# Attention in pairs of heads, and a shorter clamp in the MLP, for a sliding-window attention + hard-swish MLP kernel

## The chip, the cores and the metric

The kernel runs on one core of a Trainium2 chip. Its time is the device time of one execution in microseconds (us). Each kernel was executed several times, and the text quotes the median. All runs compared here are fast; one run of the kernel before, at 1180.69 us, was not, and is left out. The profile is of one execution; its span (first to last instruction) is about 2 us below the time of that same execution.

Engine names: PE does matmuls and transposes (PEld is its weight load), DVE is the vector engine, ACT the scalar engine, POOL the GpSimd engine; SP's queue issues the loads. SBUF and PSUM are the two on-chip memories in which the kernel allocates tiles; its matmuls write to PSUM.

## The reference, cut to what matters

Attention of 8 batches x 8 heads, 576 positions, head size 64, each position seeing itself and the 127 before it, with a linear bias per head. Then an MLP (512 to 2048 to 512) on the 4608 tokens.

```python
scores = scale * q @ k.T                         # scale = 1/8
rel = pos[:, None] - pos[None, :]
mask = (rel >= 0) & (rel < 128)
scores = np.where(mask, scores - slopes[h] * abs(rel), -1e9)
attn = softmax(scores)
x = (attn @ v)                                   # then [tokens, heads * 64]
h = x @ w_in
g = h * np.clip(h + 3.0, 0.0, 6.0) / 6.0
out = g @ w_out
```

## The kernel before

Weights, biases (`add_tiles`, which also hold the mask) and the attention's result `xT` stay in SBUF. The sequence is cut into five tiles of 128 positions (the last has 64). Scores are computed transposed (keys on partitions), so that the exponentials can be weights of the value matmul; the softmax's sum comes from a column of ones beside v. The kernel is written one head at a time. A scheduler takes the program and builds an order of instructions for each engine, so the order that runs is not the order in the text.

```python
for b in range(B):
    for h in range(H):
        ...                                             # tiles qT kT vv ldf ldb (3 buffers), tps (2, PSUM)
        nc.vector.memset(vv[:, :], 1.0)                 # for the column of ones
        for kt_i in range(n_qt):
            nc.sync.dma_start(out=ldf[:sk, 0:D], in_=q[b, h, slc, :])         # k and v likewise
            nc.vector.tensor_scalar(out=ldb[:sk, 0:D], in0=ldf[:sk, 0:D], scalar1=scale, ...)
            nc.vector.tensor_copy(out=ldb[:sk, D:2 * D], in_=ldf[:sk, D:2 * D])
            nc.vector.tensor_copy(out=vv[:sk, ds(kt_i * (D + 1), D)], in_=ldf[:sk, 2 * D:3 * D])
            nc.tensor.transpose(tps[:, :sk], ldb[:sk, 0:D], ident[:sk, :sk])
            nc.vector.tensor_copy(out=qT[:, slc], in_=tps[:, :sk])
            ...                                         # the same for kT
        for qt in range(n_qt):
            for kt_i in ([qt] if qt == 0 else [qt - 1, qt]):
                nc.tensor.matmul(sc_ps[:sk, :sq], lhsT=kT[:, kslc], rhs=qT[:, qslc], ...)
                nc.vector.tensor_tensor(out=sc_ps[:sk, :sq], in0=sc_ps[:sk, :sq], in1=at, op=ALU.add)
                nc.scalar.activation(out=exp_sb[:sk, :sq], in_=sc_ps[:sk, :sq], func=ACT.Exp)
                nc.tensor.matmul(av_ps[:sq, :], lhsT=exp_sb[:sk, :sq], rhs=vv[...], ...)
            nc.vector.reciprocal(recip[:sq, :], av_ps[:sq, D:D + 1])
            nc.vector.tensor_scalar(out=av_sb[:sq, :], in0=av_ps[:sq, :D], scalar1=recip[:sq, :], ...)
            nc.tensor.transpose(avT_ps[:, :sq], av_sb[:sq, :], ident[:sq, :sq])
            nc.vector.tensor_copy(out=xT[...], in_=avT_ps[:, :sq])
...
for nt in range(n_nt):                                  # 9 token tiles of 512
    for ms in range(n_ms):                              # 16 slices of the hidden layer
        ...                                             # 4 matmuls into hT_ps
        nc.scalar.activation(out=r6, in_=hT_ps, func=ACT.Relu, bias=bias3[:, 0:1])
        nc.vector.tensor_scalar(out=r6, in0=r6, scalar1=6.0, scalar2=1.0 / 6.0, op0=ALU.min, op1=ALU.mult)
        nc.vector.tensor_tensor(out=gT, in0=hT_ps, in1=r6, op=ALU.mult)
        ...                                             # 4 matmuls, gT into the four out_ps
```

The softmax here doesn't subtract the row's maximum and nothing guards it: scores larger than these inputs give would overflow.

## Time and profile before

| | kernel before |
|---|---|
| time, median of 11 runs | 962.65 us (960.84 to 964.21) |
| span of the profiled run | 961.8 us |
| loads of weights, to the first transpose | 36.8 us |
| attention, first transpose to first MLP matmul | 650.4 us |
| MLP, to the last copy of a result | 271.7 us |
| tail | 2.9 us |
| DVE instructions per pair of heads | 100 |

Read the stages first. Attention is two thirds of the time, and DVE is the busiest engine there; in the MLP it is PE. A total over the run (PE 77%, DVE 74%) hides that. The lines are shown in the prediction.

To split DVE's time into work and waiting I use the trace's start times, not the durations, because neighbouring DVE instructions overlap. For each kind and shape of instruction, the lower quarter point of the gaps from its start to the next start is taken as its own cost; what a gap has beyond that is counted as waiting of the next instruction. In the 300 us from 100 to 400 us the kernel before has 200.7 us of own work and 99.3 of waiting over 29.6 heads: per two heads 13.6 and 6.7 us.

### The profile page before, as it was taken

Reading aid. Unit: us, or ns where it says so; the run is one execution under the profiler, and the core shown is the slowest. Engines: PE = TensorE matmul, PEld = TensorE weight load, DVE = VectorE, ACT = ScalarE, POOL = GpSimd, SP = SyncE. Lnnn points to the kernel's source line nnn. Section 1 sums busy time; section 2 is a strip of 40 time slices with the busy share of each in tenths; the row PEclk is TensorE's granted clock in tenths of the full one; section 3 lists DMA queues with packets and bytes.
Section 4 is the critical chain, followed back from the end, with each engine's and each line's share of the span. In section 5 each row is a group of like instructions: output and inputs, shape, how many; then the busy total and the mean of one; then the engine's idle time right before and its main releaser. Section 6 shows DMA issues by size and latency. Waiting matters only on the chain.

```text
span 961.8 us, 13507 instructions
## 1 busy us (share of the span) xinstructions
PE 743.8 (77%) x3264; PEld 342.0 (36%) x3264; DVE 713.6 (74%) x3563; ACT 249.6 (26%) x721; POOL 5.1 (1%) x24
## 2 busy tenths in 40 slices
PE   0277776777777777777777777777899999999996
PEld 0133333333333333333333333333333333333332
DVE  4577887888787887878887878888556666656665
ACT  0122221222222222222222222222233333433332
POOL 2000000000000000000000000000000000000000
PEclk9999999999999999999999999999999999999999
DMA  6421222122211221222222212221001111001111
GB/s 253 125 49 41 44 45 45 44 49 45 44 43 43 46 46 40 47 45 47 44 45 48 45 44 46 45 48 39 13 0 45 45 44 44 27 18 44 45 44 44
DMA packets 134094, 47.05 MB, mean 49 GB/s; under 512 B 126848, under 2 KB 126848, under 8 KB 133504
## 3 DMA queue, kind: packets, MB, share of 16 engines
q1 hardware_dynamic: 134016, 46.20, 18.6%
q8 instruction: 25, 0.41, 0.2%
q14 instruction: 53, 0.43, 0.2%
HBM read 36.70 MB, written 9.44 MB: 48 GB/s over the span
## 4 chain that ended last, share of the span: by engine, by line
PE 48%; DVE 31%; ACT 7%; issue 6%; DMA 6%; POOL 0%; DVEq 0%; SPq 0%; ACTq 0%; POOLq 0%
PE out_ps L181 14%; PE sc_ps L133 7%; DVE sc_ps L138 7%; PE av_ps L141 7%; PE avT_ps L152 6%; PE hT_ps L170 6%; PE tps L118 4%; ACT exp_sb L140 4%; PE tps L116 4%; DVE xT L153 4%; DVE qT L117 3%; DVE gT L179 3%; ACT r L175 3%; DVE kT L119 3%; DVE av_sb L148 2%
## 5 line engine op out<-in xcount | busy, mean ns | idle before, releaser
L140 ACT ACTIVATE exp_sb<-sc_ps 128x128 bf16<-128x128 f32 (+2 forms) x576 | 149.4, 264 | 500.6 <-DVE sc_ps L138 423.5
L141 PE MATMUL av_ps<-vv,exp_sb 128*128 128x65 bf16 (+2 forms) x576 | 138.2, 241 | 67.6 <-ACT exp_sb L140 55.9
L138 DVE TENSOR_TENSOR sc_ps<-sc_ps,add_tiles 128x128 f32<-128x128 f32 (+2 forms) x576 | 155.8, 275 | 34.0 <-PE sc_ps L133 23.5
L133 PE MATMUL sc_ps<-qT,kT 64*128 64x128 bf16 (+2 forms) x576 | 154.7, 274 | 23.4 <-DVE kT L119 10.9
L181 PE MATMUL out_ps<-w_out_sb,gT 128*128 128x512 bf16 x576 | 151.5, 381 | 5.0 <-DVE gT L179 1.4
L170 PE MATMUL hT_ps<-xT,w_in_sb 128*128 128x512 bf16 x576 | 151.4, 384 | 0.3 <-DVE xT L153 0.3
L175 ACT ACTIVATE r<-hT_ps,bias 128x512 f32<-128x512 f32 x144 | 98.9, 687 | 168.6 <-PE hT_ps L170 161.4
L116 PE MATMUL tps<-ident,ldb 128*64 128x128 bf16 (+1 forms) x320 | 95.3, 303 | 59.9 <-DMA ldf<-in_k_dram 36.8
L176 DVE TENSOR_SCALAR r<-r 128x512 f32<-128x512 f32 x144 | 60.4, 421 | 84.6 <-ACT r L175 83.9
L152 PE MATMUL avT_ps<-ident,av_sb 128*64 128x128 bf16 (+1 forms) x320 | 96.9, 303 | 31.7 <-DVE av_sb L148 29.6
L141 PEld LDWEIGHTS <-exp_sb 128*128 128x128 bf16 (+2 forms) x576 | 62.7, 109 | 151.2 <-ACT exp_sb L140 119.0
L118 PE MATMUL tps<-ident,ldb 128*64 128x128 bf16 (+1 forms) x320 | 90.8, 289 | 24.2 <-DVE qT L117 13.9
L179 DVE TENSOR_TENSOR gT<-hT_ps,r 128x512 bf16<-128x512 f32 x144 | 99.4, 691 | 13.3 <-DVE r L176 0.5
L153 DVE COPY xT<-avT_ps 64x128 bf16<-64x128 bf16 (+1 forms) x320 | 66.8, 209 | 34.0 <-PE avT_ps L152 23.9
L133 PEld LDWEIGHTS <-kT 64*128 64x128 bf16 (+1 forms) x576 | 59.0, 103 | 78.3 <-DVE kT L119 30.8
L148 DVE TENSOR_SCALAR av_sb<-av_ps,recip 128x64 bf16<-128x64 f32 (+1 forms) x320 | 86.0, 269 | 0.5
L170 PEld LDWEIGHTS <-w_in_sb 128*128 128x128 bf16 x576 | 56.9, 99 | 69.8 <-issue 3.3
L181 PEld LDWEIGHTS <-gT 128*128 128x128 bf16 x576 | 46.2, 97 | 95.7 <-DVE gT L179 58.5
L119 DVE COPY kT<-tps 64x128 bf16<-64x128 bf16 (+1 forms) x320 | 65.4, 206 | 18.7 <-PE tps L118 12.1
L117 DVE COPY qT<-tps 64x128 bf16<-64x128 bf16 (+1 forms) x320 | 65.4, 205 | 14.9 <-PE tps L116 9.8
L116 PEld LDWEIGHTS <-ldb 128*64 128x64 bf16 (+1 forms) x320 | 40.8, 128 | 95.8 <-DVE ldb L110 77.9
L152 PEld LDWEIGHTS <-av_sb 128*64 128x64 bf16 (+1 forms) x320 | 40.6, 127 | 76.3 <-DVE av_sb L148 58.7
(22 smaller groups left out, 327.5 us busy)
## 6 DMA issues: line engine op xcount, KB each, us to landing
out_dram<-osb SPq DMA_DIRECT2D x36, 256.0 KB, 2.2
ldf<-in_q_dram SPq DMA_DIRECT2D x256, 32.0 KB, 1.8
ldf<-in_k_dram SPq DMA_DIRECT2D x256, 32.0 KB, 1.8
ldf<-in_v_dram SPq DMA_DIRECT2D x256, 32.0 KB, 1.9
tmp<-in_moe_w_in_dram SPq DMA_DIRECT2D x4, 1024.0 KB, 8.0
tmp<-in_moe_w_out_dram SPq DMA_DIRECT2D x16, 256.0 KB, 3.7
ldf<-in_q_dram SPq DMA_DIRECT2D x64, 16.0 KB, 1.9
ldf<-in_k_dram SPq DMA_DIRECT2D x64, 16.0 KB, 1.9
```

What stands on the lines that cost most here:

```text
L116: nc.tensor.transpose(tps[:, :sk], ldb[:sk, 0:D], ident[:sk, :sk])
L118: nc.tensor.transpose(tps[:, :sk], ldb[:sk, D:2 * D], ident[:sk, :sk])
L133: nc.tensor.matmul(sc_ps[:sk, :sq], lhsT=kT[:, kslc], rhs=qT[:, qslc], start=True, stop=True)
L138: nc.vector.tensor_tensor(out=sc_ps[:sk, :sq], in0=sc_ps[:sk, :sq], in1=at, op=ALU.add)
L140: nc.scalar.activation(out=exp_sb[:sk, :sq], in_=sc_ps[:sk, :sq], func=ACT.Exp)
L141: nc.tensor.matmul(av_ps[:sq, :], lhsT=exp_sb[:sk, :sq], rhs=vv[:sk, ds(kt_i * (D + 1), D + 1)], start=first_mm, stop=(kt_i == qt))
L152: nc.tensor.transpose(avT_ps[:, :sq], av_sb[:sq, :], ident[:sq, :sq])
L153: nc.vector.tensor_copy(out=xT[p_off:p_off + D, ds(h_off + qt * QT, sq)], in_=avT_ps[:, :sq])
L170: nc.tensor.matmul(hT_ps, lhsT=w_in_sb[:, ds(ks * d_ff + ms * 128, 128)], rhs=xT[:, ds(ks * Ntok + nt * NT, NT)], start=(ks == 0), stop=(k ...
L175: nc.scalar.activation(out=r6, in_=hT_ps, func=ACT.Relu, bias=bias3[:, 0:1])
L179: nc.vector.tensor_tensor(out=gT, in0=hT_ps, in1=r6, op=ALU.mult)
L181: nc.tensor.matmul(out_ps[sub], lhsT=gT[:, ts(sub, 128)], rhs=w_out_sb[:, ts(ms, d_model)], start=(ms == 0), stop=(ms == n_ms - 1))
```

## The change

Its intent is to halve the number of small DVE instructions: two heads share each load, cast, transpose, score add, exponential, reciprocal, scaling and copy. The value part of a query tile is written one tile later ("late"), so that the scheduler has something to put in the gaps. In the MLP, scale and bias of the Relu do part of the clamp, and the rest goes into one instruction with the product: min(relu(h/6 + 0.5), 1) x h.

```diff
-            for h in range(H):
-                qT = ap.tile([D, S], BF16)
-                vv = ap.tile([128, n_qt * (D + 1)], BF16)
-                ldf = ap.tile([128, 3 * D], FP32)
-                tps = pp.tile([D, 128], BF16)
+            for hp in range(H // 2):
+                h0 = 2 * hp
+                qT = ap.tile([128, S], BF16)
+                vv = ap.tile([128, n_qt, 2, D + 1], BF16)
+                ldf = ap.tile([128, 3, 2, D], FP32)
+                tps = ppt.tile([128, 128], BF16)            # one buffer now (cut: kT, ldb)
...
-                    nc.sync.dma_start(out=ldf[:sk, 0:D], in_=q[b, h, slc, :])
+                        nc.sync.dma_start(out=ldf[:sk, _t, :, :],
+                                          in_=src[b, h0:h0 + 2, slc, :].rearrange("h s d -> s h d"))
...
-                        sc_ps = pp.tile([128, 128], FP32)
-                        nc.tensor.matmul(sc_ps[:sk, :sq], lhsT=kT[:, kslc], rhs=qT[:, qslc],
-                                         start=True, stop=True)
+                        sc_ps = ppsc.tile([128, 2, 512], FP32)
+                        for _h in range(2):
+                            po = _h * D
+                            nc.tensor.matmul(sc_ps[:sk, _h, :sq],
+                                             lhsT=kT[po:po + D, kslc],
+                                             rhs=qT[po:po + D, qslc],
+                                             start=True, stop=True)
...
-                        nc.vector.tensor_tensor(out=sc_ps[:sk, :sq], in0=sc_ps[:sk, :sq],
+                        nc.vector.tensor_tensor(out=sc_ps[:sk, :, :sq], in0=sc_ps[:sk, :, :sq],
                                                 in1=at, op=ALU.add)
...
+                    late.append(value)                      # value(): matmuls, reciprocal, scaling,
+                    while len(late) > 1:                    # transpose and copy of one query tile
+                        late.pop(0)()
...
-                nc.scalar.activation(out=r6, in_=hT_ps, func=ACT.Relu, bias=bias3[:, 0:1])
-                nc.vector.tensor_scalar(out=r6, in0=r6, scalar1=6.0, scalar2=1.0 / 6.0,
-                                        op0=ALU.min, op1=ALU.mult)
+                nc.scalar.activation(out=r6, in_=hT_ps, func=ACT.Relu,
+                                     bias=bias3[:, 0:1], scale=1.0 / 6.0)
-                nc.vector.tensor_tensor(out=gT, in0=hT_ps, in1=r6, op=ALU.mult)
+                nc.vector.scalar_tensor_tensor(out=gT, in0=r6, scalar=1.0, in1=hT_ps,
+                                               op0=ALU.min, op1=ALU.mult)
```

More of the change, by code (lines that the diff above doesn't have):

```diff
@@ L48 @@
     bias3 = perm.tile([128, 1], FP32)
-    nc.vector.memset(bias3, 3.0)
+    nc.vector.memset(bias3, 0.5)
     make_identity(nc, ident)
@@ L93 @@
     with tc.tile_pool(name="attn", bufs=3) as ap, \
-         tc.tile_pool(name="psum", bufs=2, space=bass.MemoryType.PSUM) as pp:
-        for b in range(B):
-            for h in range(H):
-                qT = ap.tile([D, S], BF16)
-                kT = ap.tile([D, S], BF16)
-                vv = ap.tile([128, n_qt * (D + 1)], BF16)
-                ldf = ap.tile([128, 3 * D], FP32)
-                ldb = ap.tile([128, 2 * D], BF16)
-                tps = pp.tile([D, 128], BF16)
-                nc.vector.memset(vv[:, :], 1.0)
+         tc.tile_pool(name="psum", bufs=2, space=bass.MemoryType.PSUM) as pp, \
+         tc.tile_pool(name="psc", bufs=2, space=bass.MemoryType.PSUM) as ppsc, \
+         tc.tile_pool(name="ptp", bufs=1, space=bass.MemoryType.PSUM) as ppt:
+        late = []
+        add3 = add_tiles[:, :].rearrange("p (t s) -> p t s", s=128)
+        for b in range(B):
+            for hp in range(H // 2):
+                h0 = 2 * hp
+                qT = ap.tile([128, S], BF16)
+                kT = ap.tile([128, S], BF16)
+                vv = ap.tile([128, n_qt, 2, D + 1], BF16)
+                ldf = ap.tile([128, 3, 2, D], FP32)
+                ldb = ap.tile([128, 2, 2 * D], BF16)
+                tps = ppt.tile([128, 128], BF16)
+                nc.vector.memset(vv[:, :, :, :], 1.0)
                 for kt_i in range(n_qt):
@@ L106 @@
                     slc = ds(kt_i * QT, sk)
-                    nc.sync.dma_start(out=ldf[:sk, 0:D], in_=q[b, h, slc, :])
-                    nc.sync.dma_start(out=ldf[:sk, D:2 * D], in_=k[b, h, slc, :])
-                    nc.sync.dma_start(out=ldf[:sk, 2 * D:3 * D], in_=v[b, h, slc, :])
-                    nc.vector.tensor_scalar(out=ldb[:sk, 0:D], in0=ldf[:sk, 0:D],
+                    for _t, src in enumerate((q, k, v)):
+                        nc.sync.dma_start(out=ldf[:sk, _t, :, :],
+                                          in_=src[b, h0:h0 + 2, slc, :].rearrange("h s d -> s h d"))
+                    nc.vector.tensor_scalar(out=ldb[:sk, 0, :], in0=ldf[:sk, 0, :, :].rearrange("p h d -> p (h d)"),
                                             scalar1=scale, scalar2=0.0,
                                             op0=ALU.mult, op1=ALU.add)
-                    nc.vector.tensor_copy(out=ldb[:sk, D:2 * D], in_=ldf[:sk, D:2 * D])
-                    nc.vector.tensor_copy(out=vv[:sk, ds(kt_i * (D + 1), D)],
-                                          in_=ldf[:sk, 2 * D:3 * D])
-                    nc.tensor.transpose(tps[:, :sk], ldb[:sk, 0:D], ident[:sk, :sk])
+                    nc.vector.tensor_copy(out=ldb[:sk, 1, :], in_=ldf[:sk, 1, :, :].rearrange("p h d -> p (h d)"))
+                    nc.vector.tensor_copy(out=vv[:sk, kt_i, :, 0:D], in_=ldf[:sk, 2, :, :])
+                    nc.tensor.transpose(tps[:, :sk], ldb[:sk, 0, :], ident[:sk, :sk])
                     nc.vector.tensor_copy(out=qT[:, slc], in_=tps[:, :sk])
-                    nc.tensor.transpose(tps[:, :sk], ldb[:sk, D:2 * D], ident[:sk, :sk])
+                    nc.tensor.transpose(tps[:, :sk], ldb[:sk, 1, :], ident[:sk, :sk])
                     nc.vector.tensor_copy(out=kT[:, slc], in_=tps[:, :sk])
-                h_off = (h // 2) * Ntok + b * S
-                p_off = (h % 2) * D
+                h_off = hp * Ntok + b * S
                 for qt in range(n_qt):
@@ L126 @@
                     qslc = ds(qt * QT, sq)
-                    av_ps = pp.tile([128, D + 1], FP32)
-                    first_mm = True
-                    for kt_i in ([qt] if qt == 0 else [qt - 1, qt]):
+                    kts = [qt] if qt == 0 else [qt - 1, qt]
+                    exps = []
+                    for kt_i in kts:
                         sk = min(QT, S - kt_i * QT)
                         kslc = ds(kt_i * QT, sk)
-                        sc_ps = pp.tile([128, 128], FP32)
-                        nc.tensor.matmul(sc_ps[:sk, :sq], lhsT=kT[:, kslc], rhs=qT[:, qslc],
-                                         start=True, stop=True)
+                        sc_ps = ppsc.tile([128, 2, 512], FP32)
[5 more added lines that the diff above has]
+                                             start=True, stop=True)
@@ L135 @@
                         typ = 0 if kt_i == qt else 1
-                        at = add_tiles[:sk, ds((typ * H + h) * 128, sq)]
-                        exp_sb = ap.tile([128, 128], BF16)
-                        nc.vector.tensor_tensor(out=sc_ps[:sk, :sq], in0=sc_ps[:sk, :sq],
+                        at = add3[:sk, typ * H + h0:typ * H + h0 + 2, :sq]
+                        exp_sb = ap.tile([128, 2, 128], BF16, bufs=6)
+                        nc.vector.tensor_tensor(out=sc_ps[:sk, :, :sq], in0=sc_ps[:sk, :, :sq],
@@ L139 @@
                                                 in1=at, op=ALU.add)
-                        nc.scalar.activation(out=exp_sb[:sk, :sq], in_=sc_ps[:sk, :sq], func=ACT.Exp)
-                        nc.tensor.matmul(av_ps[:sq, :], lhsT=exp_sb[:sk, :sq],
-                                         rhs=vv[:sk, ds(kt_i * (D + 1), D + 1)],
-                                         start=first_mm, stop=(kt_i == qt))
-                        first_mm = False
-                    recip = ap.tile([128, 1], FP32)
@@ L146 @@
-                    nc.vector.reciprocal(recip[:sq, :], av_ps[:sq, D:D + 1])
-                    av_sb = ap.tile([128, D], BF16)
-                    nc.vector.tensor_scalar(out=av_sb[:sq, :], in0=av_ps[:sq, :D],
-                                            scalar1=recip[:sq, :], scalar2=0.0,
-                                            op0=ALU.mult, op1=ALU.add)
-                    avT_ps = pp.tile([D, 128], BF16)
-                    nc.tensor.transpose(avT_ps[:, :sq], av_sb[:sq, :], ident[:sq, :sq])
@@ L153, with value @@
-                    nc.vector.tensor_copy(
-                        out=xT[p_off:p_off + D, ds(h_off + qt * QT, sq)],
-                        in_=avT_ps[:, :sq])
+                        nc.scalar.activation(out=exp_sb[:sk, :, :sq], in_=sc_ps[:sk, :, :sq],
+                                             func=ACT.Exp)
+                        exps.append((kt_i, sk, exp_sb))
+                    def value(exps=exps, qt=qt, sq=sq, vv=vv, h_off=h_off):
+                        av_ps = pp.tile([128, 2, D + 1], FP32, name="av_ps")
+                        for _h in range(2):
+                            for i, (kt_i, sk, exp_sb) in enumerate(exps):
+                                nc.tensor.matmul(av_ps[:sq, _h, :], lhsT=exp_sb[:sk, _h, :sq],
+                                                 rhs=vv[:sk, kt_i, _h, :],
+                                                 start=(i == 0), stop=(i == len(exps) - 1))
+                        recip = ap.tile([128, 2, 1], FP32, name="recip")
+                        nc.vector.reciprocal(recip[:sq, :, :], av_ps[:sq, :, D:D + 1])
+                        av_sb = ap.tile([128, 2, D], BF16, name="av_sb")
+                        nc.vector.tensor_tensor(out=av_sb[:sq, :, :], in0=av_ps[:sq, :, :D],
+                                                in1=recip[:sq, :, :].broadcast_to([sq, 2, D]), op=ALU.mult)
+                        avT_ps = ppt.tile([128, 128], BF16, name="avT_ps")
+                        nc.tensor.transpose(avT_ps[:, :sq], av_sb[:sq, :, :].rearrange("p h d -> p (h d)"),
+                                            ident[:sq, :sq])
+                        nc.vector.tensor_copy(out=xT[:, ds(h_off + qt * QT, sq)], in_=avT_ps[:, :sq])
@@ L157 @@
+                    late.append(value)
+                    while len(late) > 1:
+                        late.pop(0)()
+                while late:
+                    late.pop(0)()
     NT = 512
```

## The prediction

> **What bounds the kernel now.** I read the page's totals first, then a table of busy time by stage, the groups split by shape, the waits, and two stretches of the timeline. The totals:
>
> ```profile
> PE 743.8 (77%) x3264; PEld 342.0 (36%) x3264; DVE 713.6 (74%) x3563; ACT 249.6 (26%) x721; POOL 5.1 (1%) x24
> ```
>
> Taken alone they name no bound. The table by stage (stretch in us, its length, then busy time and count of PE, PE's weight loads, DVE, ACT and POOL, tensor clock, DMA share, GB/s) splits the run in two:
>
> ```profile
> 100.00:660.00 560.00, 416.32 (x1835) 207.44 (x1835) 454.46 (x2777) 129.88 (x500) 0.00 (x0) 1.00 0.20 45
> 700.00:962.00 262.00, 250.99 (x1107) 98.11 (x1105) 166.02 (x313) 94.81 (x138) 0.00 (x0) 0.99 0.10 37
> ```
>
> To 37.2 us the weights load. From there to 687.2 us is attention, 64 heads in 650.0 us; the MLP's nine token tiles follow, 29.38 us apart, to 951.6 us, and a tail of 10.2 us. In attention VectorE (DVE) is busy 81% of the time, PE 74%; in the MLP PE is busy 96% and DVE 63%. So the attention change must be read on DVE, the MLP change on PE.
>
> In attention DVE does 50 instructions a head; 2777 of them in 560 us make a head every 10.08 us. They are small:
>
> ```profile
> L138 DVE TENSOR_TENSOR sc_ps<-sc_ps,add_tiles 128x128 f32<-128x128 f32 x448 | 127.2, 289 | 21.0 <-PE sc_ps L133 13.6 <-PE av_ps L141 0.7 <-ACT exp_sb L140 0.7
> L148 DVE TENSOR_SCALAR av_sb<-av_ps,recip 128x64 bf16<-128x64 f32 x256 | 69.0, 270 | 0.5
> L117 DVE COPY qT<-tps 64x128 bf16<-64x128 bf16 x256 | 54.0, 211 | 8.0 <-PE tps L116 3.6
> L114 DVE CAST vv<-ldf 128x64 bf16<-128x64 f32 x256 | 46.3, 183 | 1.4 <-DMA ldf<-in_v_dram 0.6
> L146 DVE RECIPROCAL recip<-av_ps 128x1 f32<-128x1 f32 x256 | 41.4, 162 | 8.9 <-PE av_ps L141 4.9
> ...
> L138 DVE TENSOR_TENSOR sc_ps<-sc_ps,add_tiles 128x64 f32<-128x64 f32 x64 | 14.3, 224 | 3.5 <-PE sc_ps L133 1.9 <-PE avT_ps L152 0.5
> ```
>
> The mean of one is not what it costs the queue, since neighbours overlap. Start to start, where the next was ready, the trace has about 0.20 us for a 128x128 add (0.14 at 128x64), 0.10 for a 64-element cast, 0.14 for a 128-wide PSUM copy, 0.085 for a reciprocal, 0.19 for the scaling, 0.245 for the memset. Summed over a head: casts 15 x 0.10 = 1.5, qT/kT 1.33, adds 7 x 0.20 + 2 x 0.14 = 1.68, reciprocals 0.43, scalings 0.96, xT 0.90, memset 0.25; together 7.05 us. The other 3.0 us of the 10.08 are waits of this engine, on PE for the most part:
>
> ```profile
> DVE xT L153 <- PE avT_ps L152: 23.9, 86, 0.6
> DVE sc_ps L138 <- PE sc_ps L133: 23.5, 90, 0.7
> DVE kT L119 <- PE tps L118: 12.1, 40, 0.4
> DVE qT L117 <- PE tps L116: 9.8, 42, 0.4
> ```
>
> In the MLP the timeline (start us, us, engine, line, in brackets the idle time before and its releaser) shows what PE waits for, in every group of 24 matmuls:
>
> ```profile
> 701.05 2.32 PE L170 MATMUL hT_ps<-xT,w_in_sb 128*128 128x512 bf16 x10
> 701.47 0.69 ACT L175 ACTIVATE r<-hT_ps,bias 128x512 f32<-128x512 f32 x1 [3.13 <-PE hT_ps L170]
> 702.19 0.43 DVE L176 TENSOR_SCALAR r<-r 128x512 f32<-128x512 f32 x1 [2.07 <-ACT r L175]
> ...
> 702.72 0.69 DVE L179 TENSOR_TENSOR gT<-hT_ps,r 128x512 bf16<-128x512 f32 x1
> ...
> 703.46 0.55 PEld L181 LDWEIGHTS <-gT 128*128 128x128 bf16 x4 [0.59 <-DVE gT L179]
> ```
>
> The first of the ten ends its tile's sum at about 701.26 us; gT is ready 2.2 us later. The ten matmuls are through at 703.2, so PE stands nearly 0.3 us; with two shorter waits, 24 matmuls take 5.55 us.
>
> **What the Trainium skill says.** (1) "VectorE: DVE Perf Modes", the perf-mode tier table: a cast from fp32 in SBUF runs two elements a cycle, anything fp32 with a PSUM operand one. The trace agrees: casts of 512 and 2048 elements take 426 and 1227 ns, 0.52 ns an element; adds of 64 and 128 take 224 and 289 ns, 1.02 ns. (2) The same page, the TRN2 errata: each instruction pays a fixed cost, so many small tiles pay it often. It agrees: at these slopes 110 to 160 ns of each row above is not per element. (3) "TensorE: Matmul & The Clock Gate", "Wait — 56ns, not 53.3ns?": warm matmuls of 512 columns start 215.7 ns apart. Here ten in 2.32 us of 0.384 each are 0.215 apart. (4) "ScalarE: Activation LUTs", the steps of an ACTIVATE: its scale and bias are one fused step before the lookup. So Relu with scale 1/6 should still take 0.69 us; no run here shows it yet.
>
> **The change part by part.**
>
> Heads in pairs. The built order has 50 DVE instructions for each pair instead of 100; PE has 51 matmuls a pair, each with its weight load, instead of 66 (the 15 transposes serve two heads), and the queue that issues loads has 15 instead of 30, with twice the packets each. Each instruction is wider. With the slopes above, start to start: casts 12 x 0.135 + 3 x 0.13 = 2.0 (if the strided v cast keeps two elements a cycle), qT/kT the same 1.33, since they now fill 128 partitions with the same 128 columns; adds 7 x (0.20 + 128 x 1.04 ns) = 7 x 0.335, + 2 x 0.20, = 2.75; reciprocals 0.43; scalings, now an add-like instruction of 128 elements, 5 x 0.20 = 1.0; xT 0.67; memset of 650, 0.41. Sum 8.6 us a pair, where it was 14.1. Durations should read about 0.42 us for the add, 0.215 for casts, 0.29 for scalings, and 0.38 for the exp (0.277 + 128 x 0.84 ns by ACT's own two shapes).
>
> Waits. The scores keep two buffers, each now two banks; tps and avT have one each where they had two, and "late" delays value by one query tile. I walked one steady pair in the built order by hand, with the trace's latencies: 0.40 us from the start of a transpose or score matmul to the DVE instruction that reads it, 0.11 us from one matmul to the next, 0.1 us from DVE's end to PE's start. DVE then stands about 1.0 us for qT and kT (transpose, copy, transpose on one buffer), 1.0 for xT behind other matmuls, 1.15 for score adds whose kT was only just copied, 0.35 for a reciprocal: 3.5 us, as many waits for 50 instructions as before. That makes 12.1 us a pair. The walk takes no load as late and no matmul as delayed; I add 0.6 us by judgement: 12.7 us. Attention: 32 x 12.7 = 406, and 6 us to fill and drain (before, 650.0 - 64 x 10.08 = 5) = 412 us, from 650.
>
> MLP. The min-and-scale instruction goes: 144 x 0.42 = 60 us of DVE that lies beside PE's work and is worth nothing itself. What counts is the chain: 2.2 us falls by the 0.53 from start of L176 to start of L179, to 1.67. The scheduler also reorders: now eight hT matmuls, then eight out. One ends its sum after 0.21 us of the eight, its gT comes at 0.21 + 1.67 = 1.88, the eight end at 1.72: PE stands 0.16 us per 16 matmuls, where it was 5.55 - 24 x 0.2157 = 0.37 per 24. The second gT comes at 2.74, just when it is wanted. So a token tile of 29.38 us, with 128 x 0.2157 = 27.6 in it, comes to about 28.8 (seven such waits; the groups at a tile's edge are uneven): nine make 259, where they made 264.4. That is 5 us less, not 60.
>
> Sum: 37.2 + 412 + 259 + 9.8 (the last two gT chains are shorter by 0.4) = 718 us of span; the median before is 1 us above its span, so 719.
>
> **The rivals.**
> - Same share of waits: DVE's own work falls to 8.6/14.1 = 0.61, and attention with it, 396 us: 703. For it: the kind of waits is the same. Against: fewer PSUM buffers for more work.
> - Latency takes over: with one tps and one avT the chain PE, DVE, PE sets the pace and DVE's savings turn into waits, 15 to 16 us a pair: 790 to 825. For it: the walk has DVE waiting 15 times a pair. Against: each such wait is 0.1 to 0.4 us and they already are in the 12.1.
> - Late loads: ldf is refilled five times a pair, and in the built order the third refill of q has some 2.4 us from the cast that frees it to the cast that needs it; issue takes 0.33 us or more and landing 1.8 to 1.9, now with twice the packets. If two refills a pair come 0.6 late, 1.2 us a pair: 755. For it: a wait of 0.45 us for a q load stands in the timeline at 304.70 us already.
> - PE: 476.9 us busy in attention over 64 x 33 matmuls is 0.226 each, 51 of them 11.5 us a pair, near 12.7. But that is mostly latency that nothing queues behind; two scores in a row took 0.39 us, not 0.57. I count it as a reason for waits, not a bound.
>
> **Range and chances.** The MLP and the ends are good to 6 us. Attention's period is the open term: 11.7 us (all but no extra waits) gives 687, 13.9 (late loads and some PE delay) 757. The predicted time is 719 us; I take 682 to 756. Even 18 us a pair would be 2% or more faster, so faster 0.985, same 0.01, slower 0.005.
>
> **What would show it.** Right: DVE rows halved, starts of the vv memset 12.7 us apart, the add near 420 ns, DVE busy about 75 to 80% in attention and still the busiest; token tiles 28.8 us apart, with PE waiting about 0.16 us for gT before each group of eight. Wrong: v casts near 280 ns (the strided write lost its pace), waits on DMA above 0.5 us a pair, memsets 15 us apart with DVE below 65%, or token tiles still near 29.4. The prediction fails most likely by the 0.6 us of judgement and by the walk's 3.5 us.

## The result, and the profile after

The changed kernel takes 697.59 us (median of 8 runs, 694.1 to 699.69). Its ratio to the kernel before is 0.7243 (95% interval 0.723 to 0.7256). Ratios here are the mean time of one kernel's fast runs over that of the other's in the same rounds, so they are not quite the ratio of the medians. The profiled run was the fastest of the eight, with a span of 692.2 us. All outputs are right.

| stage (profiled run) | before | after | predicted |
|---|---|---|---|
| to the first transpose | 36.8 | 35.7 | 37.2 |
| attention | 650.4 | 388.2 | 412 |
| MLP and tail | 274.6 | 268.3 | 268.8 |
| span | 961.8 | 692.2 | 718 |

Of the 269.6 us that the span lost, attention gave 262.2 and the MLP with its tail 6.3. The totals of the page after:

```profile
PE 514.7 (74%) x2784; PEld 231.2 (33%) x2784; DVE 459.8 (66%) x1819; ACT 200.5 (29%) x433; POOL 5.2 (1%) x24
```

The number of DVE instructions fell by half. The table by stage, with the columns that the prediction explains, for a part of attention and for the MLP:

```profile
100.00:400.00 300.00, 198.38 (x1278) 99.77 (x1278) 253.60 (x1254) 78.13 (x225) 0.00 (x0) 1.00 0.33 75
...
436.00:692.00 256.00, 249.36 (x1109) 98.55 (x1107) 115.92 (x175) 94.83 (x138) 0.00 (x0) 1.00 0.10 38
```

DVE is still the busiest engine of attention (253.60 of 300 us), and PE of the MLP (249.36 of 256). At 50 instructions a pair, 1254 of them are 25.1 pairs, 12.0 us each. The kernel before took 20.2 us for two heads. The groups by shape:

```profile
L144 DVE TENSOR_TENSOR sc_ps<-sc_ps,add_tiles 128x256 f32<-128x256 f32 x224 | 91.9, 428 | 9.6 <-PE sc_ps L137 3.2 <-ACT exp_sb L146 0.4 <-issue 0.2
L160 DVE TENSOR_TENSOR av_sb<-av_ps,recip 128x128 bf16<-128x128 f32 x128 | 36.3, 283 | 0.1
...
L121 DVE COPY qT<-tps 128x128 bf16<-128x128 bf16 x128 | 28.1, 220 | 1.8 <-PE tps L120 0.8
...
L119 DVE CAST vv<-ldf 128x128 bf16<-128x128 f32 x128 | 27.4, 214 | 0.6 <-DMA ldf<-in_v_dram 0.6
...
L158 DVE RECIPROCAL recip<-av_ps 128x2 f32<-128x2 f32 x128 | 20.9, 163 | 1.5 <-PE av_ps L154 0.6
L108 DVE MEMSET vv<- 128x650 bf16 x32 | 19.2, 600 | 2.7 <-DVE w_out_sb L91 0.2
```

An add over twice the elements went from 289 to 428 ns, a scaling from 270 to 283, a cast from 183 to 214, a copy from 211 to 220 and a reciprocal from 162 to 163, each at half the count. Only the memset grew nearly in proportion, from 329 ns for 325 elements to 600 for 650. DVE's waits over the whole run (total us, times, longest) are of the same kinds as before; those for scores and for xT are less than half as long in total:

```profile
DVE sc_ps L144 <- PE sc_ps L137: 10.7, 44, 0.5
DVE xT L165 <- PE avT_ps L163: 10.1, 41, 0.3
DVE recip L158 <- PE av_ps L154: 10.0, 34, 0.7
...
DVE ldb L115 <- DMA ldf<-in_q_dram: 4.5, 7, 1.1
```

The last line is new in weight: casts of q that wait for their load, up to 1.1 us.

By start times, the same 300 us hold 225.4 us of own DVE work and 74.6 of waiting: 9.0 and 3.0 us a pair, where two heads before had 13.6 and 6.7. Both fell. The waits per instruction hardly moved (3.35 us for 50 instructions before, 3.0 now), which fits half as many instructions bringing half as many waits; it is not shown, since no run changes the number alone with the order kept. The method has a flaw that matters later: where an instruction is nearly always followed by a wait, the quarter point holds part of that wait. The two 64-wide adds of a pair come out at 0.40 us start to start, when 0.20 is their likely cost (a scaling of as many elements has 0.198). With that, a pair has 8.6 us of work and 3.4 of waiting, and these are the figures to compare with kernels whose adds do not show the flaw. (The one 64-wide qT copy, 0.224 against 0.107 for kT's, shows it too, worth 0.1 us a pair more.)

The timeline in the MLP:

```profile
552.92 1.89 PE L185 MATMUL hT_ps<-xT,w_in_sb 128*128 128x512 bf16 x8
...
553.34 0.69 ACT L190 ACTIVATE r<-hT_ps,bias 128x512 f32<-128x512 f32 x1 [2.07 <-PE hT_ps L185]
554.06 0.69 DVE L193 SCALAR_TENSOR_TENSOR gT<-r,hT_ps 128x512 bf16<-128x512 f32 x1 [2.07 <-ACT r L190]
...
554.80 0.55 PEld L196 LDWEIGHTS <-gT 128*128 128x128 bf16 x4 [0.48 <-DVE gT L193]
...
556.54 1.89 PE L185 MATMUL hT_ps<-xT,w_in_sb 128*128 128x512 bf16 x8
```

There is one DVE instruction between the Relu and the matmuls that need gT, where there were two. Relu with its scale still takes 0.69 us, as the prediction took from the Trainium skill ("ScalarE: Activation LUTs", the steps of an ACTIVATE). Eight hT matmuls and eight others take 556.54 - 552.92 = 3.62 us; 16 x 0.2157 is 3.45, so PE stands 0.17 us.

### The profile page after: what moved, and what is told of

It is laid out like the page before. It is cut to its first block, busy times and chain, and to the rows that moved or that the text cites. A ratio compares the mean times of both kernels' runs of the same rounds, so it can differ in the third digit from the quotient of the medians.

```text
span 692.2 us, 9305 instructions
## 1 busy us (share of the span) xinstructions
PE 514.7 (74%) x2784; PEld 231.2 (33%) x2784; DVE 459.8 (66%) x1819; ACT 200.5 (29%) x433; POOL 5.2 (1%) x24
## 4 chain that ended last, share of the span: by engine, by line
PE 55%; DVE 22%; DMA 12%; ACT 4%; issue 4%; POOL 1%; DVEq 0%; SPq 0%; ACTq 0%; POOLq 0%
PE out_ps L196 19%; PE hT_ps L185 18%; DVE sc_ps L144 8%; PE av_ps L154 7%; DMA ldf<-in_k_dram 6%; ACT exp_sb L146 4%; DVE kT L123 4%; PE sc_ps L137 4%; PE tps L120 3%; PE tps L122 3%; DMA ldf<-in_q_dram 2%; DVE xT L165 2%; DMA tmp<-in_moe_w_out_dram 2%; PE avT_ps L163 2%; DVE ldb L118 2%
## 5 line engine op out<-in xcount | busy, mean ns | idle before, releaser
L193 DVE SCALAR_TENSOR_TENSOR gT<-r,hT_ps 128x512 bf16<-128x512 f32 x144 | 98.4, 687 | 142.5 <-ACT r L190 138.7
L146 ACT ACTIVATE exp_sb<-sc_ps 128x256 bf16<-128x256 f32 (+2 forms) x288 | 100.2, 359 | 287.4 <-DVE sc_ps L144 287.0
L154 PE MATMUL av_ps<-vv,exp_sb 128*128 128x65 bf16 (+1 forms) x576 | 94.9, 246 | 38.1 <-ACT exp_sb L146 34.5
L144 DVE TENSOR_TENSOR sc_ps<-sc_ps,add_tiles 128x256 f32<-128x256 f32 (+2 forms) x288 | 110.5, 398 | 17.1 <-PE sc_ps L137 10.7
L137 PE MATMUL sc_ps<-qT,kT 64*128 64x128 bf16 (+2 forms) x576 | 80.8, 273 | 45.6 <-ACT exp_sb L146 27.3
L120 PE MATMUL tps<-ident,ldb 128*128 128x128 bf16 (+1 forms) x160 | 43.6, 273 | 60.0 <-DMA ldf<-in_k_dram 35.7
L154 PEld LDWEIGHTS <-exp_sb 128*128 128x128 bf16 (+1 forms) x576 | 49.2, 117 | 81.3 <-ACT exp_sb L146 59.8
L122 PE MATMUL tps<-ident,ldb 128*128 128x128 bf16 (+1 forms) x160 | 42.1, 263 | 24.8 <-DVE qT L121 14.3
L163 PE MATMUL avT_ps<-ident,av_sb 128*128 128x128 bf16 (+1 forms) x160 | 45.5, 284 | 1.9 <-DVE av_sb L160 1.6
L160 DVE TENSOR_TENSOR av_sb<-av_ps,recip 128x128 bf16<-128x128 f32 (+1 forms) x160 | 45.0, 281 | 0.1
L123 DVE COPY kT<-tps 128x128 bf16<-128x128 bf16 (+1 forms) x160 | 34.6, 216 | 6.4 <-PE tps L122 1.0
```

The lines of the kernel that those rows point to most:

```text
L120: nc.tensor.transpose(tps[:, :sk], ldb[:sk, 0, :], ident[:sk, :sk])
L122: nc.tensor.transpose(tps[:, :sk], ldb[:sk, 1, :], ident[:sk, :sk])
L123: nc.vector.tensor_copy(out=kT[:, slc], in_=tps[:, :sk])
L137: nc.tensor.matmul(sc_ps[:sk, _h, :sq], lhsT=kT[po:po + D, kslc], rhs=qT[po:po + D, qslc], start=True, stop=True)
L144: nc.vector.tensor_tensor(out=sc_ps[:sk, :, :sq], in0=sc_ps[:sk, :, :sq], in1=at, op=ALU.add)
L146: nc.scalar.activation(out=exp_sb[:sk, :, :sq], in_=sc_ps[:sk, :, :sq], func=ACT.Exp)
```

## The experiments

| run | edit, in short | median us | ratio to before (95%) |
|---|---|---|---|
| e1_mlp_only | before + the MLP's change | 955.15 | 0.9938 (0.9919 to 0.9957) |
| e2_attn_only | before + attention's change | 698.76 | 0.7268 (0.7245 to 0.7291) |
| e3_no_late | after, value not delayed | 685.54 | 0.7126 (0.7114 to 0.7139) |
| e4_split_add | after, score add once per head | 713.98 | 0.742 (0.7405 to 0.7436) |
| e5_memset_pool | after, memset of vv on GpSimd | 704.75 | 0.7324 (0.731 to 0.7337) |
| e6_one_copy | after, qT and kT in one copy | 688.67 | 0.716 (0.7142 to 0.7178) |
| e7_loads | after, a load buffer per key tile | 656.46 | 0.6823 (0.6807 to 0.6839) |
| e8_mlp_lag | after, out matmuls two slices later | 683.26 | 0.7102 (0.7088 to 0.7116) |
| r1_replay_loads | after's order held, 15 load buffers | 682.76 | 0.7112 (0.7101 to 0.7123) |
| r2_replay_pool | after's order held, memset on GpSimd | 688.33 | 0.7172 (0.716 to 0.7184) |
| e9_best_late | five edits together | 612.87 | 0.6384 (0.6374 to 0.6393) |
| e10_best | the same, value not delayed | 641.64 | 0.6683 (0.6673 to 0.6693) |

The runs came in three calls, each on another chip, and in each the kernel before was run too: its median was 961.65 us beside e1 to e4, 962.15 beside e5 to e8 and 959.87 beside the last four, against 962.65 beside the changed kernel. Differences to the changed kernel below are of medians. By the ratios, which take this out, the differences of e3 to e8 change by less than 1 us, but those of r1 and r2 shrink by over 2: to 12.6 us for r1 in place of 14.8, and to 6.8 for r2 in place of 9.3.

Theory: fewer, wider DVE instructions carry attention, at a fixed cost saved per instruction, and the waits shrink with their number. Rivals: the MLP's 60 us of DVE work counts; the width alone decides, so count does not matter; late loads eat a part.

### Which part of the change carries the gain: e1, e2

e1 is the kernel before with the MLP's lines of the diff alone; e2 is the changed kernel with the MLP's lines of before.

```diff
 # e1
-    nc.vector.memset(bias3, 3.0)
+    nc.vector.memset(bias3, 0.5)
...                                                     # cut: the Relu's scale=1.0 / 6.0
-                nc.vector.tensor_scalar(out=r6, in0=r6, scalar1=6.0, ...)
-                nc.vector.tensor_tensor(out=gT, in0=hT_ps, in1=r6, op=ALU.mult)
+                nc.vector.scalar_tensor_tensor(out=gT, in0=r6, scalar=1.0, in1=hT_ps, ...)
```

> The kernel before with the MLP part of the change alone. Theory (PE bounds the MLP, only the shorter chain to gT counts): nine token tiles of 28.9 instead of 29.4 us, 4 to 5 us less than before, about 958 us. Rival (the 60 us of DVE work removed count): about 900 us.

> The changed kernel with the MLP as it was before. Theory: the token tiles go back to 29.4 us, 4 to 5 us more than the changed kernel, about 702 us, so that pairing the heads carries 260 of the 265 us. Rival (the two parts help each other, e.g. by the scheduler's order): 720 us or more.

e1 took 955.15 us, 6.5 less than the 961.65 of the kernel before, far from what the removed DVE work (60 us) would give. Its MLP stage fell from 271.7 to 264.8 us. e2 took 698.76 us. That is only 1.2 more than the changed kernel, but the stages say why: its MLP has the old 271.9 us, 6.5 more, while its attention, built in the same order, came out at 384.5 instead of 388.2 in the profiled runs. Attention varies by some us from run to run, so the MLP's part is to be read from its stage. So attention carries nearly all of the gain and the MLP some 6 us.

### The fixed cost of an instruction: e4

```diff
-                        nc.vector.tensor_tensor(out=sc_ps[:sk, :, :sq], in0=sc_ps[:sk, :, :sq],
-                                                in1=at, op=ALU.add)
+                        for _h in range(2):
+                            nc.vector.tensor_tensor(out=sc_ps[:sk, _h, :sq], in0=sc_ps[:sk, _h, :sq],
+                                                    in1=at[:, _h, :], op=ALU.add)
```

> The changed kernel with the score add of a pair split again into one add for each head, all else wide. Theory (DVE paces attention, each instruction has a fixed cost): 7 x (2 x 0.20 - 0.33) + 2 x (2 x 0.14 - 0.20) = 0.65 us a pair, 32 of them 21 us, about 718 us. Rival (waits on PE pace it and swallow DVE work): less than 5 us, 698 to 703 us.

It took 713.98 us, 16.4 more than the changed kernel for 288 more instructions of the same total width: 57 ns of time for each. The theory had 718, the rival at most 703. By start times (100 to 350 us) e4 has 9.1 us of own work a pair and 3.5 of waits, against 8.6 and 3.4 of the changed kernel: the work was added and no wait shrank to take it in. So the count costs by itself. The order was free here and is another one, so that an unknown part of the 16.4 us may be the order's. Where the four us missing from the 20 expected went is not shown, and the other merged kinds were not split singly.

### The value part's delay: e3

```diff
-                    while len(late) > 1:
+                    while len(late) > 0:
```

> The changed kernel, but the value part of each query tile is emitted at once and not one tile later. Theory (DVE's own work and as many waits set the pace, and the scheduler finds other work to put between): within 10 us of the changed kernel, 690 to 708. Rival (the delay is what hides the exp): 0.5 to 1 us more in each of 160 query tiles, 780 us or more.

It took 685.54 us, 12 less than the changed kernel and outside what was expected. So the delay, meant to help, does harm in this kernel. Its cause was not isolated: the edit gives all engines another order. e10 below shows the opposite sign.

### Less DVE work: e6, e5

e6 puts both transposes into one PSUM tile and copies them together, five copies a pair less.

```diff
-                tps = ppt.tile([128, 128], BF16)
+                tps = ppt.tile([128, 2, 128], BF16)
-                    nc.tensor.transpose(tps[:, :sk], ldb[:sk, 0, :], ident[:sk, :sk])
-                    nc.vector.tensor_copy(out=qT[:, slc], in_=tps[:, :sk])
-                    nc.tensor.transpose(tps[:, :sk], ldb[:sk, 1, :], ident[:sk, :sk])
-                    nc.vector.tensor_copy(out=kT[:, slc], in_=tps[:, :sk])
+                    nc.tensor.transpose(tps[:, 0, :sk], ldb[:sk, 0, :], ident[:sk, :sk])
+                    nc.tensor.transpose(tps[:, 1, :sk], ldb[:sk, 1, :], ident[:sk, :sk])
+                    nc.vector.tensor_copy(out=qkT[:, :, slc], in_=tps[:, :, :sk])
```

> The changed kernel with the transposes of q and k put side by side in one PSUM tile and copied out by one DVE instruction of 256 instead of two of 128. Theory: own work 1.33 - (4 x 0.21 + 0.14) = 0.35 us less a pair, and of the 1.0 us of waits that my walk gave to the chain transpose, copy, transpose about half, 0.5 us, together 0.85 x 32 = 27 us, about 671 us. If only the own work counts: 686 us. Rival (that chain is hidden by other work): the same 686 us or more.

It took 688.67 us, 8.9 less, near the second of the two readings. By start times its own DVE work is 8.2 us a pair and its waits are 3.7. Its 64-wide adds come out at 0.208 us, so it is to be set against the 8.6 and 3.4 of the changed kernel (against 9.0 and 3.0 the saving would look twice as large): 0.4 us less work (0.35 was expected) and 0.3 more waiting. Most of what DVE saved came back as waiting.

e5 gives the memset of vv to GpSimd.

```diff
-                nc.vector.memset(vv[:, :, :, :], 1.0)
+                nc.gpsimd.memset(vv[:, :, :, :], 1.0)
```

> The changed kernel with the memset of vv on GpSimd instead of DVE; nothing else reads or writes differently. Theory (DVE's own work is on the path, waits stay what they are): 0.515 us a pair off, 32 pairs 16 us, about 681 us. Rival (waits on PE set the pace and fill the gap): less than 5 us off, 693 to 698 us.

It took 704.75 us: 7 more, where both readings had expected less. The timeline of e5 around one of those memsets shows a cost that neither had:

```profile
151.98 0.64 POOL L108 MEMSET vv<- 128x650 bf16 x1 [11.35 <-PE av_ps L154]
152.00 0.70 DVE L118 CAST ldb<-ldf 128x128 bf16<-128x128 f32 x1
...
152.12 0.58 DVE L160 TENSOR_TENSOR av_sb<-av_ps,recip 64x128 bf16<-64x128 f32 x1
152.32 0.50 DVE L121 COPY qT<-tps 128x128 bf16<-128x128 bf16 x1
152.45 0.69 DVE L144 TENSOR_TENSOR sc_ps<-sc_ps,add_tiles 128x256 f32<-128x256 f32 x1
...
153.05 0.19 DVE L165 COPY xT<-avT_ps 128x64 bf16<-128x64 bf16 x1
```

The cast of k begins just after GpSimd's memset and takes 0.70 us instead of 0.214; it ends some 80 ns after the memset. The scaling, the copy and the add behind it are queued on the same engine and stretch with it. The trace has 27 such casts of 0.70 us in the 32 pairs. The Trainium skill, "SBUF — State Buffer", "Who interferes with whom", says that a DVE copy or cast in a two-port mode and a GpSimd instruction contend for a shared pair of ports, and that whichever issues first holds it for its whole instruction while the other fully blocks. The trace agrees that one of the two waits for the other to end, and it has both cases: in one pair the cast kept its 0.20 us, and there the memset took 0.79 us instead of 0.64. Which of them issued first the records can only suggest: the memset's starts 12 to 15 ns before the cast's in the 27 pairs, and 8 ns before it in this one. That pair, with the same order of DVE instructions, shows what the collision costs the queue (e5's timeline from 139.8 us, DVE alone):

```profile
139.85 0.20 DVE L118 CAST ldb<-ldf 128x128 bf16<-128x128 f32 x1
...
140.30 0.41 DVE L144 TENSOR_TENSOR sc_ps<-sc_ps,add_tiles 128x256 f32<-128x256 f32 x1
140.63 0.17 DVE L165 COPY xT<-avT_ps 128x64 bf16<-128x64 bf16 x1
```

Up to the add the starts are the same in both, counted from the cast; only the durations stretch. The xT copy then starts 1.05 us after the cast instead of 0.78, and the three after it are 0.28 to 0.34 us later too. So a collision delays the queue by some 0.3 us, not by the 0.49 that the cast is longer: 27 x 0.3 = 8 us, half of the 32 x 0.515 = 16.5 us that the memset had cost DVE. By this count 8 us should have been left; that the kernel is 7 us slower is another 15 or so, which come with its other order and waits and were not isolated.

### With the order held: r1, r2

An edit changes two things: the cost meant, and the order that the scheduler builds. To part them, the changed kernel's order on PE, DVE, ACT and the load queue was recorded from its build and replayed. A replay with nothing changed was not run on the chip, but the traces can be compared: r1 has the changed kernel's instructions in the same sequence on all four (1819 on DVE, 2784 on PE, 433 on ACT, 536 issues of loads and stores), and r2 too, but for the 32 memsets. r1 and r2 are replays with one thing changed.

```diff
 # r1: the load tile is allocated inside the loop over key tiles
-            ldf = ap.tile([128, 3, 2, D], FP32)
+                ldf = ap.tile([128, 3, 2, D], FP32, bufs=15)
 # r2
-            nc.vector.memset(vv[:, :, :, :], 1.0)
+            nc.gpsimd.memset(vv[:, :, :, :], 1.0)
```

> The changed kernel with every engine's instructions held in exactly the order that they had in it (the build shows the same sequence on PE, DVE, ACT and the load queue), but fifteen load buffers, one for each key tile, so that no load waits for a cast. It splits the 41 us that separate load buffers brought. Theory A (the order: the scheduler, planning with one buffer a pair, interleaved the pairs worse): here only the 9 us of DVE waits on loads can go, 688 to 695 us. Theory B (late loads on the chip, also behind each other in the queue): all of it goes, about 657 us.

> The changed kernel with the same order held on PE, DVE, ACT and the load queue, and only the memset of vv taken out of DVE and put on GpSimd. Theory (my walk of the order: the memset stands before a score add that cannot start earlier, since its buffer must first pass ACT and PE): 0 to 5 us off, 693 to 698 us, so that the 7 us more of the free build come from its other order. Rival (DVE's own work is all on the path): 16 us off, 681 us.

r1 took 682.76 us, 14.8 less than the changed kernel and between the two readings. Its DVE waits from 60 to 350 us have no line for a load:

```profile
DVE xT L303 <- PE avT_ps L302: 10.5, 48, 0.3
DVE recip L297 <- PE av_ps L293: 7.2, 25, 0.4
DVE sc_ps L285 <- PE sc_ps L280: 6.1, 26, 0.4
```

The changed kernel has these in the same stretch:

```profile
DVE xT L165 <- PE avT_ps L163: 7.2, 29, 0.3
...
DVE sc_ps L144 <- PE sc_ps L137: 6.1, 26, 0.4
DVE ldb L115 <- DMA ldf<-in_q_dram: 3.9, 6, 1.1
DVE ldb L118 <- DMA ldf<-in_k_dram: 1.6, 6, 0.4
```

By start times, the waits before ldb casts fall from 10.4 to 0.6 us in 300 us, 0.39 us a pair, or 12.5 us in 32 pairs. The attention stage agrees, 375.7 us in place of 388.2, and so does the ratio (12.6). So late loads did cost the changed kernel 12 to 15 us: the third rival was partly true.

r2 took 688.33 us, 9.3 less (6.8 by the ratio), for 16.5 us of DVE work taken away; this too lies between the readings. In this order most k casts begin 0.48 us after the memset's start and take 0.24 us, so the collision is nearly absent (two stretched casts in the 32 pairs). But the waits have grown:

```profile
DVE sc_ps L285 <- PE sc_ps L280: 12.7, 46, 0.3
...
DVE ldb L261 <- DMA ldf<-in_q_dram: 3.5, 7, 0.8
```

The add that used to stand behind the memset now finds its scores not ready: 12.7 us against 6.1 in the same stretch. Nearly half of the saving went there.

### The loads, with the order free: e7

```diff
-                ldf = ap.tile([128, 3, 2, D], FP32)
                 for kt_i in range(n_qt):
+                    ldf = ap.tile([128, 3, 2, D], FP32, bufs=6)
```

> The changed kernel with a load buffer for each key tile, six of them, so that no refill waits for the casts of the tile before it in the same buffer. Theory (loads are seldom late: DVE waits 9 us in all on loads): 0 to 8 us less, 690 to 698 us. Rival (late loads make part of the waits, also through the order in which the queue issues them): 0.6 us a pair, 19 us, 679 us or less.

It took 656.46 us, 41.1 less than the changed kernel, far more than either reading. r1 accounts for 14.8 us of it with the order held (12.6 by the ratio). The other 26 to 28 us come with the order that the scheduler builds once a pair's loads no longer share one tile: e7's DVE does 50 instructions in 10.9 us, 9.0 of own work as before and 1.85 of waits, where the changed kernel has 3.0. (Here the flaw of the method sits in the scalings, 0.309 us against 0.198: with these at 0.198, e7 has 2.4 us of waits against the 3.4 of the changed kernel, again 1 us less.) The windows of the changed kernel and of e7, 100 to 350 us:

```profile
100.00:350.00 250.00, 165.56 (x1069) 83.26 (x1068) 212.34 (x1048) 65.35 (x188) 0.00 (x0) 1.00 0.33 75
```

```profile
100.00:350.00 250.00, 173.86 (x1167) 95.36 (x1166) 217.21 (x1150) 73.89 (x206) 0.00 (x0) 1.00 0.37 82
```

The same time holds 1150 DVE instructions in place of 1048, at nearly the same busy time. Which property of the new order makes its waits so short was not isolated.

### PE's wait in the MLP: e8

The out matmuls of a slice are written two slices later, so gT has long been ready when PE comes to it.

```diff
+            pend = []
             for ms in range(n_ms):
                 ...
-                for sub in range(n_ks):
-                    nc.tensor.matmul(out_ps[sub], lhsT=gT[:, ts(sub, 128)], ...)
+                pend.append((ms, gT))
+                while len(pend) > 2 or (pend and ms == n_ms - 1):
+                    ms_, gT_ = pend.pop(0)
+                    for sub in range(n_ks):
+                        nc.tensor.matmul(out_ps[sub], lhsT=gT_[:, ts(sub, 128)], ...)
```

> The changed kernel with the out matmuls of the MLP emitted two steps behind the hT matmuls, so that gT has 3.4 us to come instead of 1.5. Theory (PE waits only for gT's chain, 0.16 us for every 16 matmuls): token tiles of 27.7 instead of 28.9 us, 9 to 10 us less, about 688 us. Rival (what is over 27.6 us in a tile is the edge between tiles, where out_ps is copied out): less than 3 us off.

It took 683.26 us, 5 less than expected, 14.3 less than the changed kernel by the medians and 11.0 by the profiled spans (the changed kernel's was its fastest run). The MLP stage fell from 265.4 to 254.6 us. The waits from 440 to 660 us, of the changed kernel and then of e8:

```profile
PEld L196 <- DVE gT L193: 43.7, 112, 0.8
```

```profile
PEld L200 <- DVE gT L194: 4.3, 16, 0.3
```

These are the waits of the weight loads, which run ahead of the matmuls; PE itself lost 0.15 to 0.16 us at a time in the changed kernel, seven times in a token tile. In e8 PE was busy for all 220 us of that stretch, and its token tiles are 27.73 us apart after the first. So it was the chain to gT that PE waited for, as the prediction had it.

### A version that beats both: e9, and e10

e9 takes the changed kernel with the edits of e6, e7 and e8, casts q and k in one instruction (the score's scale moves into the exponential, the bias is divided by it), and sets only the column of ones.

```diff
-                    scalar1=-slopes[h], scalar2=0.0, op0=ALU.mult, op1=ALU.add,
+                    scalar1=-slopes[h] / scale, scalar2=0.0, op0=ALU.mult, op1=ALU.add,
-                nc.vector.memset(vv[:, :, :, :], 1.0)
+                nc.vector.memset(vv[:, :, :, D:D + 1], 1.0)
-                    (scaling cast of q, cast of k)
+                    nc.vector.tensor_copy(out=ldb[:sk, :, :], in_=ldf[:sk, 0:2, :, :].rearrange("p t h d -> p t (h d)"))
-                                             func=ACT.Exp)
+                                             func=ACT.Exp, scale=scale)
```

> The changed kernel with: a load buffer for each key tile, out matmuls two steps behind, q and k cast by one instruction (the scale moves into the exp, the bias is divided by it), their transposes in one PSUM tile and copied by one instruction, the memset on the ones column only. DVE's own work falls from 9.0 to about 7.6 us a pair. If waits stay at the 1.85 us a pair of the kernel with separate load buffers: 9.5 us a pair, about 600 us; if they grow back to 3: 635 us.

> The same, with the value part emitted at once. If the 12 us of the run without the delay came from the loads (the delay keeps buffers longer): no difference to the kernel with it, within 4 us. If the delay costs by itself: about 12 us less.

e9 took 612.87 us: 36% less than the kernel before and 12% less than the changed one (612.87 / 697.59 = 0.879). Its attention takes 315.8 us and its MLP 254.7. By start times a pair costs 8.0 us of own DVE work and 1.9 of waits (with the scalings at 0.198 in place of the 0.285 found here, 7.6 and 2.3). Its window, to be set against the two above:

```profile
100.00:350.00 250.00, 184.94 (x1306) 110.60 (x1306) 214.22 (x1020) 83.47 (x232) 0.00 (x0) 1.00 0.39 89
```

e10, without the delay of the value part, took 641.64 us, 29 more, where a gain of up to 12 was expected from e3. Its own DVE work is the same; its waits are 2.8 us a pair. So the delay harms the changed kernel by 12 us and helps e9 by 29: its sign depends on the order that the rest gives.

## Why the prediction was right or wrong

The prediction was right: 697.59 us lies in its range of 682 to 756, 21 below the 719 predicted. By its steps:

- **The bound.** It held. DVE's instruction count set attention (e4: each added instruction cost 57 ns), and PE's wait for gT set what the MLP could gain (e1, e8).
- **Own work, 8.6 us a pair.** It held: 9.0 by the quarter points, 8.6 with the two 64-wide adds at 0.20. The durations named ahead came out: add 428 ns (420), casts 214 (215), scalings 283 (290), and the v cast kept its pace. The memset was mis-sized: taken as 0.41 us start to start, it was 0.515; that the sum came to 8.6 all the same is luck in part, as the casts came to 1.9 us and not 2.0. The trace before had what was needed: its one-element memset of `bias` took 59 ns and that of 325 elements 329, which is 0.83 ns an element and gives 600 ns for 650, as measured. Two readings of the working are off without consequence: of the rows shown, the scaling has 205 ns that are not per element (270 - 64 x 1.02), not 110 to 160; and xT is priced at 0.90 us a head before but at 0.67 a pair after, for copies of the same width. By the quarter points xT has 0.68 a head and 0.67 a pair, so that a head had 6.8 us of work and 3.3 of waits, not 7.05 and 3.0.
- **Waits, 3.5 us a pair.** The sum held (3.4, or 3.0 by the quarter points), its make did not, so that the sum is in part luck. Worked out by the quarter points for the 25 pairs of the 300 us: qT and kT 0.63 (walked as 1.0), xT 0.55 (1.0), score adds 0.78 (1.15), reciprocals 0.40 (0.35), the memset 0.18 and the loads' casts 0.42, neither of which the walk had. Even with the 0.4 us behind the 64-wide adds put to the matmuls, the walk was too long for those, and it was wrong to take no load as late.
- **0.6 us by judgement.** This is the step that failed in size. The walk's work and waits came to 12.1 and the chip took 12.0: the 0.6 us, 19 us over 32 pairs, were not needed. They stood for late loads and delayed matmuls. Loads did cost 0.39 us (r1), but the walk's surplus on the other waits already covered them. Attention came out 24 us shorter than predicted: 32 x 0.7 = 22 from the period, the rest from a fill of 5 us where 6 were taken.
- **The MLP, 259 us for nine tiles.** It held. Token tiles came 28.83 us apart on the mean, from last out matmul to last out matmul (28.8), and PE's wait was 0.15 to 0.17 us for 16 matmuls (0.16). The single distances alternate between 29.65 and 27.92 us (once 28.27), but not because every second tile waits less: in the built order there are 132 matmuls between the marks in one and 124 in the next, and 8 x 0.2157 is the 1.73 us between them. Every tile has seven such waits, as predicted; at 0.155 us each they are the 1.1 us that separate 28.83 from e8's 27.73.
- **The signs.** DVE rows halved, but DVE's share of attention was 253.60 / 300 = 85%, not 75 to 80, because the period was shorter. The memsets came 12.0 us apart (25 in 300 us), not 12.7.
- **The rivals.** "Same share of waits" gave 703, nearer than the prediction, but not for its reason: the share of waits was not the same, it fell from 33% to 25% of DVE's time (28% with the 64-wide adds at 0.20). "Latency takes over" fell, as waits per instruction stayed. "Late loads" was true at a third of its size (by its own 1.2 us a pair it comes to 757, not 755). The chain of PE was no bound: PE was busy 66% of attention.

What was beyond the prediction is the size of the scheduler's share. With another order, e7 shows 26 to 28 us less without any less work on DVE.

## What to carry to other kernels

Where an engine is bound by many small instructions, count them, and price each by its start-to-start time; merging two heads into one instruction saves the fixed part, and here the waits fell with it. Price by durations and you overrate a stall: in e5 four durations stretched by 0.3 to 0.5 us each, and the queue lost 0.3 us in all. Work taken off such an engine comes back in part as waiting (r2: 16.5 us of work gave 7 to 9), so look for the waits that take its place. Where a scheduler builds the order, a one-line edit is also a new order, worth tens of us in either direction: hold the order fixed before you ascribe a difference to the edit, and try variants together before you drop one.

## What the Trainium skill lacked or had wrong

- "VectorE: DVE Perf Modes", "Zero memsets can be issued as uint32 (trn2)", gives a memset one cycle per element, and the page's clock is 0.96 GHz, so 1.04 ns by estimate. Here 325 further bf16 elements took 271 ns (272 by start times), 0.83 ns each, and 650 took 600 ns in all.
- "SBUF — State Buffer", "Who interferes with whom": a cast of 0.214 us took 0.70 beside a GpSimd memset, as its rule has it; that the first to issue wins is only suggested (leads of 12 to 15 ns against 8). It doesn't say how this looks in a profile: the instructions queued behind the blocked cast stretch too, a scaling from 273 to 584 ns and a copy from 220 to 500, while their starts do not move; the queue lost some 0.3 us, not 0.49.
- No page that I read says how much a built order matters for a comparison: separate load buffers gave 41 us with the order free (e7) and 13 to 15 with it held (r1).
